# Fused q/k stack loads, a re-timed maxima chain and a new unit order in an attention + MLP kernel

## Chip, cores and metric

The kernel runs on one core of a Trainium2 chip. The metric is device time in microseconds (us), lower is better; the time of a kernel is the median over its runs. One further execution was recorded by the hardware profiler, and all rows of traces come from such an execution.

## The reference

For x of 2048 rows and 512 columns the kernel computes `g * a + (1 - g) * b`:

```
g = sigmoid((x * gate_w).sum(-1))
a = softmax(mask(q k^T / 4)) v @ wo      # q, k, v = x @ wqkv; 32 heads of 16 columns;
                                         # mask: row i sees rows i-255 .. i
b = gelu(layernorm(x) @ w1 + b1) @ w2 + b2   # w1: 512 x 1792, w2: 1792 x 512
```

## The kernel before

Every large matrix product is done in float32r (F32R) with operands split into a high part and a low remainder: `copy` (L121, on ACT) writes the high part, `lo_part` (L118, on DVE, or on POOL where asked for) the rest, and each product is three matmuls (high-high, low-high, high-low). PE is the engine of all matmuls.

Work runs in three phases.

**Phase one** makes q, k and v. `first_units` (PE L260) makes the first q and k block while its weights and x arrive; then a list of 48 *units* runs, one `tick` of a step counter for each: `qk_unit` (PE L272, 12 matmuls), one for each of 4 head groups, q or k and 4 blocks of 512 rows, and `v_unit` (PE L297, 12 matmuls), one for each of 16 blocks of 128 rows. `qk_out` splits each q or k result (ACT L121, DVE L118) and writes it to DRAM (`qkd`; L282 issued from ACT, L283 from SP). x is loaded in four blocks `load_x` (SP L216), the v weights by `load_wv` (SP L207). Beside the units the dictionary `plan` starts other things at unit numbers: `stat_unit` (row means and variances, DVE), `stat_end` (the reciprocal root by Newton steps, DVE), `load_y` and the first score blocks. `load_y` makes the normalised rows for the MLP, called y: for each half `cp` of the rows it loads 8 slices of 128x512, subtracts the mean and scales (L466, L467, on POOL), then splits (ACT L121, DVE L118). Before the change, the first half of y and half of the second are made in phase one, and four slices in phase two.

**Phase two** mixes attention with the MLP's first layer. The string `ORDER`, 1202 letters, is the program order of PE by hand: `S` is `s_pair`, scores for a block of 128 queries, two heads (PE L322), masked and reduced to row maxima by DVE (L328, or L331 and L332); `T` is `st_pair`, the transposed scores (PE L369), from which ACT takes the exponential (L371) and POOL clears what lies outside the window (`affine_select`, L373); `P` is `pv`, p times v (PE L388); `f` is one pair of matmuls of `mlp1_unit` (PE L578). Heads go by eight groups `p` of four, as two pairs `pr`; S runs six blocks (`LAG`) ahead of T. PE results of S, T, P and `mlp1_unit` share four double PSUM banks, handed round in turn (`ring`).

Two chains link these units through DRAM.

- *Stacks.* `load_stacks` (SP L309) brings 256 columns of q and k for head group p+1 from `qkd` into SBUF tiles `qs[0]`, `qs[1]`, `ks[0]`, `ks[1]`: four transfers of 98 partitions a call, 56 calls in phase two.
- *Maxima.* T needs minus the row maxima of S as two extra rows of the q stacks. After each fourth block `put_max` splits the maxima on POOL (L340 and L118, tile nm), transposes them on DVE (L345), writes them to a DRAM tile `md` (SP L346) and reads them back into the stacks (SP L353, four transfers). The split is issued at once, the transpose and the write at the next `tick`, the reads at the third; in phase two a `tick` is a `T` with `pr` 0.

DMAs are issued in program order from two queues, SP's and ACT's. The DMAs of both queues use eight completion semaphores in turn, and the issue of a DMA waits until the one that had its semaphore before is done.

**Phase three** (GELU on ACT L634, the MLP's second layer on PE L784, the output projection on PE L763, the gate on DVE L766 and L789) is not touched.

## Time and profile before

| | |
|---|---|
| runs before | 730.5, 727.93, 729.96 us; median 729.96 us |
| profiled execution | 728.15 us, its span 726.4 us, mean granted PE clock 0.995 |
| PE matmul busy | 699.0 us, 96% of the span |
| DVE, ACT, POOL busy | 472.7, 370.3, 281.1 us |
| phase one, two, three | first matmul at 6.23 us; first matmul of phase two at 156.17 us; last `P` at 510.77 us |
| DMA | 138.46 MB, mean 191 GB/s |

How to read it: busy PE time counts a matmul from its issue to its modelled end, and matmuls overlap, so 96% busy does not mean that PE runs at its best rate; what counts for a change is where PE stands idle, or issues more slowly than in a quiet stretch, and what it waited for. The granted clock (PEclk) is the share of the full TensorE clock that was granted in a stretch. Idle time of an engine other than PE costs nothing by itself.

### The profile page before, as it was taken

Reading aid. Unit: us, or ns where it says so; the run is one execution under the profiler, and the core shown is the slowest. Engines: PE = TensorE matmul, PEld = TensorE weight load, DVE = VectorE, ACT = ScalarE, POOL = GpSimd, SP = SyncE. Lnnn points to the kernel's source line nnn. Section 1 sums busy time; section 2 is a strip of 40 time slices with the busy share of each in tenths; the row PEclk is TensorE's granted clock in tenths of the full one; section 3 lists DMA queues with packets and bytes.
Section 4 is the critical chain, followed back from the end, with each engine's and each line's share of the span. In section 5 each row is a group of like instructions: output and inputs, shape, how many; then the busy total and the mean of one; then the engine's idle time right before and its main releaser. Section 6 shows DMA issues by size and latency. Waiting matters only on the chain.

```text
span 726.4 us, 16108 instructions
## 1 busy us (share of the span) xinstructions
PE 699.0 (96%) x5728; PEld 542.1 (75%) x5728; DVE 472.7 (65%) x981; ACT 370.3 (51%) x584; POOL 281.1 (39%) x612
## 2 busy tenths in 40 slices
...
GB/s 299 307 293 294 231 175 238 226 234 197 179 227 189 230 226 175 154 169 220 222 206 179 183 170 134 196 107 149 210 267 150 178 135 134 155 137 93 190 108 58
DMA packets 104675, 138.46 MB, mean 191 GB/s; under 512 B 15668, under 2 KB 55540, under 8 KB 104468
## 3 DMA queue, kind: packets, MB, share of 16 engines
...
## 4 chain that ended last, share of the span: by engine, by line
PE 78%; DMA 7%; DVE 5%; POOL 3%; SPq 2%; ACT 2%; issue 2%; ACTq 1%; DVEq 0%; POOLq 0%
PE ps_b L578 17%; PE ps_a L784 16%; PE ps_d L272 11%; PE ps_b L388 11%; PE ps_o L763 6%; PE ps_b L369 6%; PE ps_d L297 5%; PE ps_b L322 5%; DVE mx L332 2%; DMA qk<-t 2%; POOL p L373 2%; DVE ps_b L331 1%; DMA t<-in_w 1%; PE ps_d L260 1%; DMA hp<-t 1%
## 5 line engine op out<-in xcount | busy, mean ns | idle before, releaser
L373 POOL TENSOR_SCALAR_AFFINE_SELECT p<-p 128x256 f32<-128x256 f32 x480 | 184.2, 413 | 116.7 <-ACT p L371 115.0
L371 ACT ACTIVATE p<-ps_b 128x768 f32<-128x768 f32 (+2 forms) x256 | 191.3, 772 | 59.5 <-PE ps_b L369 51.7
L578 PE MATMUL ps_b<-x,w 64*128 64x512 f32 x1344 | 216.8, 398 | 0.5 <-DVE mx L332 0.4
L784 PE MATMUL ps_a<-x,t 128*128 128x512 f32 x648 | 154.6, 395 | 1.3 <-DVE t L638 1.2
L332 DVE TENSOR_REDUCE mx<-ps_b 128x2 f32<-128x512 f32 x208 | 144.1, 693 | 7.2
L784 PEld LDWEIGHTS ps_a<-x,t 128*128 128x128 f32 x648 | 121.4, 188 | 31.5 <-issue 1.6
L578 PEld LDWEIGHTS ps_b<-x,w 64*128 64x128 f32 x1344 | 132.7, 187 | 11.9 <-issue 3.6
L331 DVE COPY_PREDICATED ps_b<-tri,ps_b 128x256 f32<-128x256 uint8 x208 | 88.1, 424 | 54.9 <-PE ps_b L322 46.4
L369 PE MATMUL ps_b<-q,k 50*128 50x384 f32 (+5 forms) x512 | 91.8, 346 | 7.1 <-DVE mx L332 3.3
L272 PE MATMUL ps_d<-x,w 128*128 128x512 f32 x360 | 91.5, 404 | 3.7 <-ACT x L121 3.2
L388 PE MATMUL ps_b<-p,v 128*32 128x128 f32 (+1 forms) x1920 | 91.3, 329 | 0.7 <-ACT p L371 0.5
L322 PE MATMUL ps_b<-k,q 62*128 62x384 f32 (+2 forms) x472 | 86.9, 346 | 3.5 <-DVE mx L328 1.5
L272 PEld LDWEIGHTS ps_d<-x,w 128*128 128x128 f32 x360 | 67.9, 191 | 22.9 <-ACT x L121 4.6
L388 PEld LDWEIGHTS ps_b<-p,v 128*32 128x32 f32 x1920 | 54.1, 109 | 36.8 <-ACT p L371 4.8
L121 ACT ACTIVATE t<-ps_b 128x256 f32<-128x256 f32 (+1 forms) x114 | 52.9, 489 | 46.0 <-PE ps_b L388 35.6
L369 PEld LDWEIGHTS ps_b<-q,k 64*128 64x128 f32 (+1 forms) x512 | 52.0, 185 | 28.9 <-issue 14.4
L322 PEld LDWEIGHTS ps_b<-k,q 62*128 62x128 f32 x472 | 48.2, 186 | 17.5 <-ACT p L371 4.0
L118 DVE TENSOR_TENSOR t<-t,t 128x512 fp32r<-128x512 f32 x70 | 48.5, 692 | 14.9 <-ACT t L121 11.9
L634 ACT ACTIVATE t<-t,b1s 128x512 f32<-128x512 f32 x56 | 37.9, 715 | 25.5 <-DMA t<-hp 24.8
L121 ACT ACTIVATE t<-t 128x512 fp32r<-128x512 f32 x16 | 10.1, 632 | 76.7 <-DVE t L751 35.7
L763 PE MATMUL ps_o<-w,t 128*128 128x512 f32 x192 | 46.6, 392 | 0.6 <-ACT t L121 0.5
L297 PE MATMUL ps_d<-wv,x 128*128 128x512 f32 x192 | 46.9, 394 | 0.0
...
## 6 DMA issues: line engine op xcount, KB each, us to landing
...
k<-qk SPq DMA_DIRECT2D x112, 98.0 KB
q<-qk SPq DMA_DIRECT2D x112, 98.0 KB
...
```

Of the source, the lines that this page charges most:

```text
L272: pe.matmul(o, a[:, dt * 128:(dt + 1) * 128], b[:, dt * C:(dt + 1) * C], start=n == 0, stop=n == 11)
L297: pe.matmul(o, x[:, a:a + 128], wvs[dt][:, k], start=n == 0, stop=n == 11)
L322: pe.matmul(o[:, e, :n], qs[pr][r:k, qb * 128:qb * 128 + 128], ks[pr][r:k, t0:t0 + n], start=True, stop=True)
L331: dve.copy_predicated(o[:, :, :128], tri, o[:, :, 256:384])
L332: dve.tensor_reduce(m, o[:, :, :256], mybir.AxisListType.X, ALU.max)
L369: pe.matmul(o[:, e, :w], ks[pr][r:k, kb * 128:kb * 128 + 128], qs[pr][r:k, kb * 128:kb * 128 + w], start=True, stop=True)
L371: act.activation(pt[:, :, :w], o[:, :, :w], AF.Exp, scale=0.25)
L373: pool.affine_select(out=pt[:, :, a:a + 128], in_=pt[:, :, a:a + 128], pattern=[[0, 2], [sgn, 128]], base=b, channel_multiplier=-sgn, comp ...
L388: pe.matmul(a[32 * h:32 * h + 32, at:at + w], vs[:, kb, v:v + 32], pts[p, kb][:, h, fr:fr + w], start=n == 0, stop=n == len(parts) - 1, sk ...
L578: pe.matmul(o[:, e], w[kt // 4][r:r + 64, k, m:m + 128], y[r:r + 64, a:a + C], start=n == 0, stop=n == 23)
L763: pe.matmul(a, x[:, g], wos[g][:, k], start=n == 0, stop=n == 11)
L784: pe.matmul(accs[c][b], x[:, b * 128:(b + 1) * 128], w, start=f == 0 and n == 0, stop=f == FT - 1 and n == 2)
```

## The change

It does the following.

1. *Stacks in one tile.* The four stack tiles become one tile `qk` with four slots; `load_stacks` issues two transfers instead of four, each with both head pairs, and the maxima's reads become two instead of four.
2. *Maxima by order steps.* In phase two the four steps of `put_max` are issued 6, 11, 13 and 20 letters of `ORDER` after the `S` that completes a group of maxima (`CHAIN`, `soon`): split, transpose, write, read. In phase one they stay with the ticks.
3. *All of y in phase one.* `stat_end` is split into two halves at units 22 and 30; `load_y(0)` starts at unit 24 (31 before), `load_y(1)` with all eight slices at unit 33 (40 before, with four slices); the split of a slice comes one step later. The pool `x8` gets ten buffers instead of eight, and in phase two two of them serve as p tiles, whose pool shrinks from seven to five.
4. *Start.* The first weights come in three pieces (128, 128 and 256 columns) instead of two of 256, for q and k; twelve bf16 matmuls on a tile of zeros run on PE ahead of the first real ones; the split of x's third block (`rests[2]`), which was at unit 3, goes ahead of the first `qk_out`.
5. *Order.* `ORDER` is a new string with the same numbers of letters: 647 f, 256 T, 236 S and 63 P.
6. *Scratch.* The scratch for dynamic DMAs is halved.

The diff; of the two `ORDER` strings only the first line of each is shown, where `...` stands:

```diff
--- before.py
+++ after.py
@@ -35,20 +35,21 @@
 EPS = 1e-5
 NEG = -3.0e38
 U8 = mybir.dt.uint8
-ORDER = ("fSfTfffffTfTSfffSffTfSfffTTfffTfSfffSPSTSfffTTfffSfffTSfffTffSfTPTSffTffSffTSffSfSPTSTfffSffTfSffSPT"
...
+ORDER = ("fTSTffffffSffTfSfffTfSffTfSfffTSffffSPffSfffTSfffTfSffTfSfffTfffTSfTfffSffSPTTSPTSfffTfSffTfSfffTSff"
...
          "TT")
 LAG = 6
+CHAIN = (6, 11, 13, 20)
 
 
 @with_exitstack
@@ -131,19 +132,25 @@
         for fn in todo.pop(step[0], []):
             fn()
 
+    spot = [None]
+    soons = {}
+
+    def soon(n, fn):
+        soons.setdefault(spot[0] + n, []).append(fn)
+
     def settle():
         while todo:
             tick()
 
     osc = dram.tile([8, 128, S], F32, name="osc")
-    stat = dram.tile([2, S], F32, name="stat")
+    stat = dram.tile([2, 2, S // 2], F32, name="stat")
     hp = dram.tile([NCH, FT, 128, C], F32, name="hp")
     qkd = {(g, t): dram.tile([HG, 50, S], F32R, name=f"qk{g}_{t}") for g in range(NG) for t in range(2)}
 
     open_pool("w")
     open_pool("ring")
-    qs = [get("ring", f"q{j}", 1, (128, S), F32R) for j in range(2)]
-    ks = [get("ring", f"k{j}", 1, (128, S), F32R) for j in range(2)]
+    qk = get("ring", "qk", 1, (128, 4, S), F32R)
+    qs, ks = [qk[:, pr] for pr in range(2)], [qk[:, 2 + pr] for pr in range(2)]
     vs = get("ring", "v", 1, (128, NB, VR))
     tri = consts.tile([128, 2, 128], U8, name="tri")
     wide = consts.tile([128, 256], BF16, name="wide")
@@ -152,7 +159,7 @@
     g0 = consts.tile([128, NB], F32, name="g0")
     g1 = consts.tile([128, NB], F32, name="g1")
     mv = consts.tile([128, NB, 2], F32, name="mv")
-    rt = consts.tile([128, 2, NB], F32, name="rt")
+    rt = consts.tile([128, 2, 2, NB // 2], F32, name="rt")
 
     open_pool("edge", "right")
     get("edge", "edge", 1, (128, 8))
@@ -162,7 +169,7 @@
     gws = get("work", "gws", 1, (128, D))
 
     def x8():
-        return get("x", "x8", 8, (128, 2048), F32R)
+        return get("x", "x8", 10, (128, 2048), F32R)
 
     def wt():
         return get("w", "w", 6, (128, 2, 512), F32R)
@@ -186,6 +193,7 @@
         for e in range(2):
             pool.tensor_copy(tri[:, e], one[:, :128])
         pool.memset(wide, 0.0)
+        pool.memset(rt, 0.0)
         pool.affine_select(out=wide[:, 128:], in_=wide[:, 128:], pattern=[[-1, 128]], base=0, channel_multiplier=1,
                            compare_op=ALU.is_ge, fill=NEG)
 
@@ -238,18 +246,25 @@
             wq[0, t] = w
             ws.append(w)
             raws.append(t2())
-        for a in range(2):
+        pieces = (slice(0, 128), slice(128, 256), slice(256, 512))
+        for k in pieces:
             for t in range(2):
-                act.dma_start(raws[t][:, a * 256:a * 256 + 256], wqk[0, t, :, a * 256:a * 256 + 256])
+                act.dma_start(raws[t][:, k], wqk[0, t, :, k])
         _, hi, lo = load_x(0)
+        idle = t2()
+        dve.memset(idle, 0.0)
+        idle = idle.bitcast(BF16)
+        o = two()[:, 0]
+        for _ in range(12):
+            pe.matmul(o, idle[:, :128], idle[:, :512], start=True, stop=True)
         masks()
         loads()
         for t in range(2):
             os.append(ps("d"))
         for dt in range(DT):
             for t in range(2):
-                if dt % 2 == 0:
-                    k = slice(dt * 128, dt * 128 + 256)
+                if dt < 3:
+                    k = pieces[dt]
                     copy(ws[t][:, 0, k], raws[t][:, k])
                     lo_part(ws[t][:, 1, k], raws[t][:, k], ws[t][:, 0, k])
                 if t == 0:
@@ -260,6 +275,7 @@
                     pe.matmul(os[t], ws[t][:, k, dt * 128:dt * 128 + 128], x[:, dt * C:dt * C + C],
                               start=dt == 0 and n == 0, stop=dt == DT - 1 and n == 2)
         rests[1]()
+        rests[2]()
         for t in range(2):
             qk_out(0, t, 0, os[t])
 
@@ -303,10 +319,9 @@
     def load_stacks(p, a, n):
         g, j = divmod(p, 2)
         held_cols[p] = a + n
-        for pr in range(2):
-            for t, dst in ((1, ks[pr]), (0, qs[pr])):
-                src = view(qkd[g, t], [S, 98], [1, n], off=(4 * j + 2 * pr) * 50 * S + a)
-                sp.dma_start(f32(dst[14:112, a:a + n]), f32(src))
+        for t in (1, 0):
+            src = view(qkd[g, t], [S, 98], [100 * S, 2], [1, n], off=4 * j * 50 * S + a)
+            sp.dma_start(f32(qk[14:112, 2 * t:2 * t + 2, a:a + n]), f32(src))
 
     mxs, done = {}, set()
 
@@ -337,23 +352,31 @@
         mx = mxs[p][:, :, :, a:a + 4]
         m = small("nm", 2, (128, 2, 2, 2, 4), F32R)
         ms = small("ms", 2, (128, 32))
-        pool.tensor_copy(m[:, 0], mx)
-        lo_part(m[:, 1], mx, m[:, 0], pool)
         md = dram.tile([2, 2, 2, 4, 128], F32R, name=nm("md"))
+
+        def parts():
+            pool.tensor_copy(m[:, 0], mx)
+            lo_part(m[:, 1], mx, m[:, 0], pool)
 
         def turn():
             dve.transpose(ms, f32(m).rearrange("p a b c d -> p (a b c d)"))
+
+        def put():
             sp.dma_start(f32(view(md, [32, 4], [128, 32], [1, 32])), ms)
 
         def rest():
             done.add(("m", p, a // 4))
-            for pr in range(2):
-                for e in range(2):
-                    src = view(md, [2048, 2], [1, 512], off=(2 * pr + e) * 512)
-                    sp.dma_start(f32(qs[pr][62 + 50 * e:64 + 50 * e, a * 128:a * 128 + 512]), f32(src))
-
-        after(1, turn)
-        after(2 if (p, a) == (7, 12) else 3, rest)
+            for k in range(2):
+                src = view(md, [512, 2], [1024, 2], [1, 512], off=2048 * k)
+                sp.dma_start(f32(qk[62 + k:113 + k:50, :2, a * 128:a * 128 + 512]), f32(src))
+
+        if spot[0] is None:
+            parts()
+            after(1, lambda: (turn(), put()))
+            after(3, rest)
+        else:
+            for n, fn in zip(CHAIN, (parts, turn, put, rest)):
+                soon(n, fn)
 
     pts, acc = {}, {}
 
@@ -361,7 +384,7 @@
         w = min(NB - kb, 3) * 128
         assert ("m", p, (kb * 128 + w - 1) // 512) in done
         if pr == 0:
-            pts[p, kb] = get("work", "p", 7, (128, 4, 384))
+            pts[p, kb] = p_tile()
         pt = pts[p, kb][:, 2 * pr:2 * pr + 2]
         o = two()
         for e in range(2):
@@ -419,12 +442,13 @@
 
         after(3, rest)
 
-    def stat_end():
-        ve = small("ve", 1, (128, NB))
-        u = small("u", 1, (128, NB))
-        r = rt[:, 1, :]
+    def stat_end(half):
+        ve = small("ve", 2, (128, NB // 2))
+        u = small("u", 2, (128, NB // 2))
+        m = mv[:, half * 8:half * 8 + 8]
+        r = rt[:, half, 1]
         ri = r.bitcast(I32)
-        dve.tensor_scalar(ve, mv[:, :, 1], EPS, None, op0=ALU.add)
+        dve.tensor_scalar(ve, m[:, :, 1], EPS, None, op0=ALU.add)
         dve.tensor_scalar(ri, ve.bitcast(I32), 1, None, op0=ALU.logical_shift_right)
         dve.tensor_scalar(ri, ri, -1.0, float(0x5f3759df), op0=ALU.mult, op1=ALU.add)
         for _ in range(4):
@@ -432,10 +456,12 @@
             dve.tensor_tensor(out=u, in0=u, in1=ve, op=ALU.mult)
             dve.tensor_scalar(u, u, -0.5, 1.5, op0=ALU.mult, op1=ALU.add)
             dve.tensor_tensor(out=r, in0=r, in1=u, op=ALU.mult)
-        dve.tensor_copy(rt[:, 0, :], mv[:, :, 0])
+        dve.tensor_copy(rt[:, half, 0], m[:, :, 0])
         s = small("ms", 2, (128, 32))
-        dve.transpose(s, rt.rearrange("p a b -> p (a b)"))
+        dve.transpose(s, rt.rearrange("p h a b -> p (h a b)"))
         sp.dma_start(view(stat, [32, 4], [128, 32], [1, 32]), s)
+        if not half:
+            return
         for g, sgn in ((g0, -1.0), (g1, 1.0)):
             act.activation(g, z, AF.Exp, scale=sgn)
 
@@ -452,7 +478,7 @@
         mr = [t2() for _ in range(2)]
         for j in range(2):
             for e in range(2):
-                sp.dma_start(mr[j][64 * e:64 * e + 64], view(stat, [0, 64], [1, C], off=j * S + (2 * cp + e) * C))
+                sp.dma_start(mr[j][64 * e:64 * e + 64], view(stat, [0, 64], [1, C], off=cp * S + j * 2 * C + e * C))
 
         def one(s):
             if (cp, 0, s // 4) not in ys:
@@ -472,7 +498,7 @@
                 done.add(("y", cp, s))
 
             after(lag, rest)
-            after(lag + 2, fin)
+            after(lag + 3, fin)
 
         for s in range(s0, s1):
             after(1 + (s - s0) * gap // 2, lambda s=s: one(s))
@@ -519,7 +545,6 @@
     def at(n, fn):
         plan.setdefault(n, []).append(fn)
 
-    at(3, rests[2])
     for dt in range(DT):
         at(4 + dt // 2, rests["v"][dt])
     at(6, rests[3])
@@ -532,11 +557,12 @@
         at((4, 6, 8, 12)[c], lambda c=c: load_stacks(0, c * C, C))
     for i in range(NB):
         at(11 + i, lambda i=i: stat_unit(i))
-    at(30, stat_end)
+    at(22, lambda: stat_end(0))
+    at(30, lambda: stat_end(1))
     for n, (g, t) in enumerate((g, t) for g in range(1, NG) for t in range(2)):
         at((6, 7, 9, 10, 12, 13)[n], lambda g=g, t=t: after(3, load_w(g, t)))
-    at(31, lambda: load_y(0, 0, KT, 3, pool))
-    at(40, lambda: load_y(1, 0, KT // 2, 3, pool))
+    at(24, lambda: load_y(0, 0, KT, 3, pool))
+    at(33, lambda: load_y(1, 0, KT, 3, pool))
     at(41, lambda: load_w1(0, dve))
     at(44, lambda: load_w1(1, dve))
     for qb in range(NB - LAG):
@@ -556,12 +582,19 @@
     nt[0] = 9
     open_psum({"b0": 1, "b1": 1}, {"b2": 1, "b3": 1})
     ring += ["b0", "b1", "b2", "b3"]
+    extra = [f32(x8())[:, :1536].rearrange("p (h n) -> p h n", h=4) for _ in range(2)]
+    np_ = [0]
+
+    def p_tile():
+        np_[0] += 1
+        n = np_[0] % 7
+        return extra[n // 4] if n in (3, 6) else get("work", "p", 5, (128, 4, 384))
+
     late = []
 
     jobs = [(f, cp) for cp in range(2) for f in range(3)] + [(f, cp) for f in range(3, FT - 2) for cp in range(2)]
     jobs += [(f, cp) for cp in range(2) for f in range(FT - 2, FT)]
     load_w1(2)
-    after(1, lambda: load_y(1, KT // 2, KT, 2, pool, 4))
 
     def mlp1_unit(f, cp):
         held = ring.pop(0)
@@ -665,12 +698,16 @@
             early.extend(load_h(0, f) for f in range(2))
 
     early = []
+    spot[0] = 0
     lt = [(p, kb, pr) for p in range(8) for kb in range(NB) for pr in range(2)]
     ls = [(p, qb, pr) for p in range(8) for qb in range(NB) for pr in range(2)][2 * (NB - LAG):]
     lp = [(p, j) for p in range(8) for j in range(NB // 2)]
 
     def run(order):
         for a in order:
+            spot[0] += 1
+            for fn in soons.pop(spot[0], []):
+                fn()
             flush()
             if a == "T":
                 p, kb, pr = lt.pop(0)
@@ -818,7 +855,7 @@
 
 
 def build():
-    nc = bacc.Bacc("TRN2", target_bir_lowering=False, num_devices=1, dynamic_dma_scratch_size=1024)
+    nc = bacc.Bacc("TRN2", target_bir_lowering=False, num_devices=1, dynamic_dma_scratch_size=512)
 
     def inp(name, shape):
         return nc.dram_tensor(name, list(shape), F32, kind="ExternalInput").ap()
```

22 lines of the change are left out of this document (11 added, 11 removed).

## The prediction

> **What bounds the kernel now.** I read the page first, then stretches of phase two.
>
> ```profile
> span 726.4 us, 16108 instructions
> PE 699.0 (96%) x5728; PEld 542.1 (75%) x5728; DVE 472.7 (65%) x981; ACT 370.3 (51%) x584; POOL 281.1 (39%) x612
> ...
> 40.00:60.00 20.00, 20.00 (x89) 15.90 (x88) 7.52 (x20) 5.57 (x11) 3.55 (x2) 1.00 0.89 286
> 160.00:250.00 90.00, 82.85 (x960) 62.47 (x962) 65.36 (x148) 60.61 (x94) 61.30 (x144) 0.98 0.67 204
> 250.00:500.00 250.00, 246.56 (x3030) 189.72 (x3032) 185.32 (x416) 178.54 (x275) 147.82 (x392) 1.00 0.58 180
> 230.00:235.00 5.00, 2.50 (x14) 2.53 (x16) 1.12 (x2) 1.78 (x4) 3.00 (x6) 0.77 0.58 170
> 235.00:240.00 5.00, 5.00 (x61) 3.71 (x60) 2.92 (x7) 2.54 (x5) 1.93 (x7) 0.89 0.82 244
> ```
>
> PE is the bound: of 726.4 us it stands idle for 27.4. The change takes no real matmul away, so it can win only where PE idles or runs slowly. Phase one has no such place once it runs (20.00 of 20.00 busy from 40 to 60). The start has one (part 4). The first quarter of phase two is the other: from 160 to 250 PE idles 90 - 82.85 = 7.15 us; from 250 to 500 only 3.44 us, or 1.24 us for 90. So 5.9 us of idling are peculiar to the early stretch. Its granted clock is lower too: 5 x (1 - 0.77) + 5 x (1 - 0.89) = 1.70 us are lost between 230 and 240. Together 7.6 us. By matmuls the gap is larger: at the later pace (3030 in 250 us) 90 us would hold 1091, and 960 were issued; 131 missing at 12.1 per us are 10.8 us. So the early stretch offers 7.6 to 10.8 us.
>
> **Part 1: y leaves phase two.** The chain of waits from 155 to 190 us, by line:
>
> ```profile
> by line: POOL p L373 21.6%; DVE mx L332 12.9%; DVE x L118 8.3%; DVE ps_b L331 8.0%; POOL t L467 7.3%; POOL t L466 7.1%; issue 6.0%; PE ps_b L369 4.8%; PE ps_b L388 4.1%; PE ps_d L297 4.1%; POOL w L118 3.6%; PE ps_b L322 3.1%; PE ps_b L578 2
> ```
>
> PE has hardly a fifth of this chain. Scaling of y (L466, L467) and y's split (DVE x) hold 7.1 + 7.3 + 8.3 = 22.7% of 35 us, 7.9 us, ahead of the masking on which T and S wait. They go, with their four loads. PE cannot win all of it, since exponentials and maxima come next on the chain: it can win its 5.9 us of idling less the 2.9 of part 2, so 3.0, and by the matmul count up to 10.8 less the 4.6 of part 2, so 6.2. I take 4.5, the middle.
>
> The price is paid by DVE and POOL in phase one.
>
> ```profile
> 60.83 2.97 PE ps_d L272 x12
> 69.94 2.98 PE ps_d L272 x12
> ...
> L118 DVE TENSOR_TENSOR x<-t,x 128x512 fp32r<-128x512 f32 x5 | 8.1, 1636 | 1.1 <-ACT x L121 1.1
> L332 DVE TENSOR_REDUCE mx<-ps_x 128x2 f32<-128x512 f32 x4 | 2.8, 693 | 0.1
> L118 DVE TENSOR_TENSOR t<-ps_d,t 128x512 fp32r<-128x512 f32 x4 | 2.7, 686 | 5.1 <-ACT t L121 5.1
> L331 DVE COPY_PREDICATED ps_x<-tri,ps_x 128x256 f32<-128x256 uint8 x4 | 1.7, 419 | 0.0
> ```
>
> Three units and two score blocks take 69.94 - 60.83 = 9.11 us, a unit 3.04. The groups are DVE's from 120 to 140 us, while POOL works on y: y's split takes 1.64 us there, the same operation from PSUM 0.69. After the change a slice of y is due in each unit from 30 to 47, and DVE has for each 1.64 + 2/3 x 0.69 + 2/3 x (0.69 + 0.42) = 2.84 us of work in 3.04. It fits with 0.2 us to spare, and four PSUM banks of results hide a delay of two units. So nothing is charged; the second `stat_end` half, some twenty tiny DVE operations, has the same cover. If it is gone, see the rivals. y's twelve loads a half pass SP earlier, among the writes of q and k parts (L283) and the row loads of `stat_unit`; each waits for a free t tile, and behind it stand q and k writes that PE needs only in phase two.
>
> The Trainium skill's page "SBUF — State Buffer", section "Who interferes with whom", speaks against this move: a DVE instruction with two SBUF inputs and a GpSimd instruction that reads SBUF exclude each other. The trace agrees: 1636 ns against 686 ns with one input in PSUM.
>
> **Part 2: the maxima chain.** One group came late:
>
> ```profile
> 220.96 0.69 DVE L332 TENSOR_REDUCE mx<-ps_b 128x2 f32<-128x512 f32 x1
> 222.75 0.60 SPq L346 DMA_DIRECT2D md<-ms  x1
> 228.09 1.51 SPq L353 DMA_DIRECT2D q<-md  x4
> 232.50 0.68 PE L369 MATMUL ps_b<-q,k 64*128 64x384 f32 x2 [2.87 <-DMA q<-md]
> ...
> SPq L346 <- DVE ps_b L331: 29.6, 17, 5.1
> 156.17 0.50 PE L578 MATMUL ps_b<-x,w 64*128 64x512 f32 x2
> 510.77 1.72 PE ps_b L388 x32
> ```
>
> The maximum is done at 221.65 and its write issued at 222.75, but the reads only at 228.09, two ticks and a busy SP queue later; T waits 2.87 us. In the new order the reads stand seven letters behind the write. The 1202 letters take 510.77 - 156.17 = 354.6 us, 0.295 us each, so seven are 2.1 us instead of 5.3. The same T also stands 46 letters behind its S instead of 33 (counted in the strings). So the 2.9 us go, and the 1.7 us of low clock behind them: 4.6. What comes late next is ordinary bank waiting. The other steps move little: the split now queues behind a few `affine_select`s on POOL, the transpose is issued two letters ahead of the write, which shortens SP's 29.6 us of standing at L346 with all later transfers behind it. Those are off PE's path today. The reads, only 2.1 us behind the write, will often stand in SP until it has landed; behind them wait the results of the MLP (hp), w1 and the next stacks, for a microsecond or two that SP's fewer issues make good.
>
> **Part 3: half the stack transfers.**
>
> ```profile
> k<-qk SPq DMA_DIRECT2D x112, 98.0 KB
> 421.18 3.65 DMA q<-qk
> PE ps_b L322 <- DMA q<-qk: 0.5, 1, 0.5
> ```
>
> In phase two 112 stack issues and about 60 reads of maxima leave SP; bytes stay. PE waited only 0.5 us for a stack, so there is little to win, and the new order spends the room: from each `load_stacks` to the first S that needs it I add up letters (0.18 us for S and T, 0.23 for f, 1.44 for P, from the spacing of their matmuls). The shortest lead falls from 5.7 to 4.7 us, and 14 of 56 loads have at most 7 us (2 before). A load of half the size held the chain for 3.65 us: inside, not by much. I charge 0.5 us.
>
> **Part 4: the start.**
>
> ```profile
> 6.23 7.93 PE L260 MATMUL ps_d<-x,w 128*128 128x512 f32 x24 [6.23 <-ACT x L121]
> 22.95 8.24 PE L272 MATMUL ps_d<-x,w 128*128 128x512 f32 x24 [3.20 <-ACT x L121]
> 31.03 5.74 PE L297 MATMUL ps_d<-wv,x 128*128 128x512 f32 x24
> ...
> 22.27 2.19 ACT L121 ACTIVATE x<-v 128x512 fp32r<-128x512 f32 x4 [3.05 <-issue]
> 30.31 1.16 ACT L121 ACTIVATE wv<-t 128x512 fp32r<-128x512 f32 x2 [1.26 <-issue]
> ...
> 26.00:28.00 2.00, 2.00 (x6) 1.60 (x5) 0.17 (x2) 0.80 (x2) 0.00 (x0) 0.52 0.79 225
> ```
>
> Twenty-four matmuls take 5.74 us at 31.03, but 7.93 at 6.23, and 8.24 at 22.95, where the clock falls to 0.52 after a wait of 3.2. The dummies can give at most 7.93 - 5.74 = 2.2 us, the moved cast 3.2 + 8.24 - 5.74 = 5.7. But ACT is serial here: the v weights are split at 30.31 behind q and k copies and DMA issues, and PE takes them up at 31.03. An earlier PE waits there. ACT itself gains at most the 3.05 us that it lost at 22.27, less its standing for x's third block ahead of the first `qk_out`, which it delays. The finer first weights put two more issues on ACT, and two of x's first slices then wait for one of the eight semaphores; that may cost as much as the smaller first piece wins. So I take 1.5 us, the middle of 4 gained (3.05 and something of the dummies' 2.2) and 1 lost (two issues and a late slice).
>
> The Trainium skill ("TensorE: Matmul & The Clock Gate", Part 1) says that the clock is halved by default and freed by some 3.4 us of steady work. By that rule alone the dummies would bring their whole 2.2 us. The trace agrees in kind with the 0.52 after a wait.
>
> The halved scratch costs nothing: the DMA groups are issued by SP or ACT.
>
> **The sum**, against the profiled 728.15 us (the span and 1.75 around it): 4.5 (y) + 4.6 (maxima) - 0.5 (loads) + 1.5 (start) = 10.1 saved, 718.0. The median, 729.96, is 1.8 above that execution; I set the forecast of the median between, at 719.
>
> **Rivals.** *Everything pays in full*: 10.8 early in phase two, 4 at the start, 728.15 - 14.8 = 713. SP's 29.6 us of standing speak for it, ACT's serial start against. *DVE bounds phase one*, the SBUF page's rule taken at its word: if 18 units run 0.3 us over their 3.04, 5.4 us go back: 724. It decides once DVE needs more than 3.04 us a unit for longer than the banks cover. *Loads land late*, the slower side: if a double load needs 7 us, the 14 close ones stall 0 to 2.3 us, some 1.6 each, 22 us: 718 + 22 = 740. It begins where a landing passes 4.7 us; 3.65 at half size speaks against it, SP's standing for it. *The one tile ties what was apart*, so that transfers aren't really moved out of PE's way: if a load counts as covering all columns between its two halves, the next T waits for it, 56 x 3.65 = 204 us: 922. No row speaks for it.
>
> **How the numbers follow.** Forecast 0.55, full gain 0.15, DVE-bound 0.13, late loads 0.13, tied tile 0.04. Half a percent, 3.65 us, is about what a measurement can tell: faster means below 726.3. Forecast, full gain and most of DVE-bound lie there, 0.80; the mild end of late loads gives no change, 0.07; slower 0.13. The range of 710 to 729 holds the first three, with the ends of the early stretch and the start, and that mild end.
>
> **What would show it.** Right: from 160 to 250 PE idles about 2 us at clock 1.00; PE has no wait for q<-md; L466 and L467 end before phase two; the 1202 letters take about 346 us; the 3.2 us wait for x gives way to one for wv. Wrong: PE waits for q<-qk or k<-qk of over 5 us in sum; PE gaps on ps_d in units 30 to 47; a first matmul of phase two later than 156.17.

## The result, and the profile after

The changed kernel takes 747.7 us (median of 4 runs, 745.93 to 749.54) against 728.94 beside it: a ratio of 1.0256, 95% interval 1.0221 to 1.0292. The forecast was 719 and "faster". It is slower by 18.8 us, on the side to which the prediction gave 0.13; none of its rivals gives this time.

The page of the kernel after, and its busy time by stretches (us, then PE, PEld, DVE, ACT, POOL with their instructions, PE's granted clock, DMA share, GB/s):

```profile
span 746.6 us, 15926 instructions
PE 705.5 (94%) x5740; PEld 548.0 (73%) x5740; DVE 481.2 (64%) x1006; ACT 370.4 (50%) x585; POOL 280.8 (38%) x613
...
100.00:120.00 20.00, 15.38 (x57) 11.49 (x56) 12.71 (x24) 3.72 (x8) 11.97 (x9) 0.84 0.76 245
120.00:140.00 20.00, 15.61 (x61) 11.96 (x60) 18.39 (x41) 5.92 (x10) 9.28 (x10) 0.90 0.54 157
160.00:250.00 90.00, 88.17 (x956) 68.95 (x956) 64.90 (x144) 61.06 (x96) 49.59 (x123) 1.00 0.67 201
250.00:500.00 250.00, 238.43 (x2907) 184.70 (x2908) 180.52 (x408) 170.68 (x265) 141.82 (x377) 0.99 0.59 181
```

The same two stretches of phase one in the kernel before:

```profile
100.00:120.00 20.00, 20.00 (x90) 15.41 (x89) 14.43 (x46) 4.49 (x9) 1.41 (x3) 1.00 0.65 194
120.00:140.00 20.00, 20.00 (x90) 15.40 (x89) 13.75 (x17) 7.16 (x13) 19.45 (x15) 1.00 0.66 194
```

PE is idle 41.1 us instead of 27.4 (span less busy time). It idles in two new places of phase one, where before it never paused: 90 matmuls in 20 us became 57 and 61. From 250 to 500 its idling went from 3.44 to 11.57 us. What it waited for, longest sums first:

```profile
PE ps_x L337 <- DVE mx L347: 9.0, 4, 4.0
PE ps_b L392 <- DMA qk<-md: 8.7, 3, 4.5
PE ps_d L313 <- ACT wv L122: 6.6, 2, 4.6
PE ps_b L337 <- DMA qk<-qk: 6.2, 5, 2.5
```

Four places, one for each part of the prediction: banks of score blocks (ps_x) that DVE hadn't emptied in phase one (part 1), maxima read late (part 2), split v weights (part 4), stacks (part 3).

The profiled execution (748.36 us, against 728.15) is cut up below at the start of the thirteenth block of twelve matmuls ("start"), at phase two's first matmul, and at its last P. The later kernels are explained with their experiments.

| kernel | start | to phase two | the 1202 letters | rest |
|---|---|---|---|---|
| before | 48.5 | 107.7 | 354.6 | 215.7 |
| after | 51.6 | 121.7 | 358.5 | 214.8 |
| u_cast | 48.4 | 122.2 | 356.5 | 215.1 |
| early_stat | 50.9 | 108.2 | 359.7 | 214.4 |
| old_ticks | 51.0 | 123.5 | 348.6 | 213.9 |
| mix | 49.0 | 109.7 | 351.2 | 215.0 |
| s_new | 48.7 | 109.9 | 363.4 | 216.0 |
| s_letters | 48.2 | 111.3 | 360.7 | 213.9 |
| s_ticks | 48.7 | 110.1 | 363.7 | 215.0 |
| s_y | 47.9 | 109.4 | 353.6 | 213.3 |

So the 20.2 us of the two profiled executions are 3.1 (start) + 14.0 (the rest of phase one) + 3.9 (the letters) - 0.8 (the rest). Of the 14.0, 9.0 are the waits for ps_x; the lower clock of 100 to 140 us, 20 x (1 - 0.84) + 20 x (1 - 0.90) = 5.2 us, makes up the rest. Kernels with the order and the steps of the kernel after and all of y in phase one take from 356.5 (u_cast) to 366.3 us (short_lags, below) for the letters. One profile's figure in that column therefore says little below 10 us.

### The profile page after: what moved, and what is told of

Same layout as the page of the kernel before. It is cut to its first block, busy times and chain, and to the rows that moved or that the text cites. A ratio compares the mean times of both kernels' runs of the same rounds, so it can differ in the third digit from the quotient of the medians.

```text
span 746.6 us, 15926 instructions
## 1 busy us (share of the span) xinstructions
PE 705.5 (94%) x5740; PEld 548.0 (73%) x5740; DVE 481.2 (64%) x1006; ACT 370.4 (50%) x585; POOL 280.8 (38%) x613
## 4 chain that ended last, share of the span: by engine, by line
PE 74%; DMA 11%; DVE 6%; SPq 4%; ACT 2%; issue 1%; ACTq 1%; POOL 0%; DVEq 0%
PE ps_b L611 19%; PE ps_a L821 16%; PE ps_b L411 11%; PE ps_d L288 7%; PE ps_b L392 6%; PE ps_b L337 6%; PE ps_o L800 5%; PE ps_d L313 5%; DMA qk<-qk 4%; DMA t<-in_xa 2%; DMA qk<-md 1%; ACTq L298 1%; DMA v<-in_xt 1%; DMA md<-ms 1%; DMA hp<-t 1%
## 5 line engine op out<-in xcount | busy, mean ns | idle before, releaser
L396 POOL TENSOR_SCALAR_AFFINE_SELECT p<-p 128x256 f32<-128x256 f32 x344 | 131.7, 411 | 108.2 <-ACT p L394 97.6
L394 ACT ACTIVATE p<-ps_b 128x768 f32<-128x768 f32 (+2 forms) x184 | 137.5, 770 | 53.5 <-PE ps_b L392 49.7
L346 DVE COPY_PREDICATED ps_b<-tri,ps_b 128x256 f32<-128x256 uint8 x208 | 88.5, 425 | 68.0 <-PE ps_b L337 51.6
L392 PE MATMUL ps_b<-qk 64*128 64x384 f32 (+5 forms) x512 | 90.0, 342 | 8.9 <-DMA qk<-md 8.7
L337 PE MATMUL ps_b<-qk 62*128 62x384 f32 (+3 forms) x472 | 85.6, 344 | 7.6 <-DMA qk<-qk 6.2
L411 PE MATMUL ps_b<-p,v 128*32 128x256 f32 (+1 forms) x1376 | 74.6, 329 | 0.7 <-ACT p L394 0.7
L392 PEld LDWEIGHTS ps_b<-qk 64*128 64x128 f32 (+1 forms) x512 | 51.8, 186 | 25.8 <-issue 14.3
L396 POOL TENSOR_SCALAR_AFFINE_SELECT x<-x 128x256 f32<-128x256 f32 x136 | 52.3, 411 | 42.3 <-ACT x L394 41.3
L394 ACT ACTIVATE x<-ps_b 128x768 f32<-128x768 f32 (+2 forms) x72 | 54.8, 777 | 18.5 <-PE ps_b L392 11.5
L337 PEld LDWEIGHTS ps_b<-qk 62*128 62x128 f32 (+1 forms) x472 | 47.5, 186 | 21.7 <-issue 11.0
L119 DVE TENSOR_TENSOR t<-t,t 128x512 fp32r<-128x512 f32 x70 | 48.5, 693 | 14.6 <-ACT t L122 10.9
L313 PE MATMUL ps_d<-wv,x 128*128 128x512 f32 x192 | 50.9, 417 | 6.6 <-ACT wv L122 6.6
L313 PEld LDWEIGHTS ps_d<-wv,x 128*128 128x128 f32 x192 | 38.6, 202 | 17.0 <-ACT wv L122 8.0
```

What stands on the lines that cost most here:

```text
L313: pe.matmul(o, x[:, a:a + 128], wvs[dt][:, k], start=n == 0, stop=n == 11)
L337: pe.matmul(o[:, e, :n], qs[pr][r:k, qb * 128:qb * 128 + 128], ks[pr][r:k, t0:t0 + n], start=True, stop=True)
L346: dve.copy_predicated(o[:, :, :128], tri, o[:, :, 256:384])
L392: pe.matmul(o[:, e, :w], ks[pr][r:k, kb * 128:kb * 128 + 128], qs[pr][r:k, kb * 128:kb * 128 + w], start=True, stop=True)
L394: act.activation(pt[:, :, :w], o[:, :, :w], AF.Exp, scale=0.25)
L396: pool.affine_select(out=pt[:, :, a:a + 128], in_=pt[:, :, a:a + 128], pattern=[[0, 2], [sgn, 128]], base=b, channel_multiplier=-sgn, comp ...
```

## The experiments

Line numbers shift by a few between kernels. Eleven kernels have a single run each. The time of the kernel before that was measured beside it is 727.84 (u_cast, u_start, u_y, sp_first), 725.44 (short_lags, ticks, four, old_order) or a median of 727.49 (early_stat, old_ticks, wide).

### Undo one part of the start, or y's schedule

`u_cast` puts the cast of x's third block back:

```
         rests[1]()
-        rests[2]()
...
+    at(3, rests[2])
```

> The changed kernel with the cast of x's third block (rests[2]) back at unit 3; all else as changed. In the changed kernel the seventh block of twelve matmuls starts 1.9 us earlier than before the change, and the eighth 3.2 us later, which then stays. Theory A (the moved cast delays the first q and k writes on ACT, PE runs ahead, waits 4.6 and 2.0 us for the v weights and then runs at half clock): the 3.2 us go, and with the dummies' gain the eighth block starts 0 to 1 us ahead of before; the first matmul of phase two comes 3 to 4 us earlier than 173.3, about 169.7; total 744.5. Rival B (the finer first weights and the two more issues on ACT cost it): the eighth block stays about 3 us late, phase two starts at 173, total 748.

Measured 743.89. PE in the kernel after:

```profile
7.28 6.08 PE L275 MATMUL ps_d<-x,w 128*128 128x512 f32 x24 [1.59 <-ACT x L122]
13.20 11.36 PE L288 MATMUL ps_d<-x,w 128*128 128x512 f32 x48
29.12 1.32 PE L313 MATMUL ps_d<-wv,x 128*128 128x512 f32 x2 [4.56 <-ACT wv L122]
32.44 8.20 PE L313 MATMUL ps_d<-wv,x 128*128 128x512 f32 x22 [2.00 <-ACT wv L122]
```

and in u_cast:

```profile
7.24 6.07 PE L275 MATMUL ps_d<-x,w 128*128 128x512 f32 x24 [1.29 <-ACT x L122]
23.20 8.54 PE L287 MATMUL ps_d<-x,w 128*128 128x512 f32 x24 [4.28 <-ACT x L122]
31.57 5.75 PE L312 MATMUL ps_d<-wv,x 128*128 128x512 f32 x24
```

With the cast moved up, PE runs 48 matmuls through (13.20 to 24.56), then stands 4.56 and 2.00 us for the v weights, and the 22 matmuls behind that take 8.20 us where 24 take 5.75 (the granted clock was 0.50 from 32.4 to 36.5). The wait has moved behind the next block and grown from 4.3 to 6.6 us. Why the weights come late is in ACT's row of work in the kernel after:

```profile
17.11 1.25 ACTq L298 DMA_DIRECT2D qk<-t  x2
...
24.89 3.50 ACTq L298 DMA_DIRECT2D qk<-t  x2
28.44 1.15 ACT L122 ACTIVATE wv<-t 128x512 fp32r<-128x512 f32 x2 [3.58 <-DMA qk<-t]
...
31.76 1.15 ACT L122 ACTIVATE wv<-t 128x512 fp32r<-128x512 f32 x2 [1.69 <-issue]
```

ACT casts first, so its first q and k writes go out at 17.11; in u_cast they do so at 14.13. Then two issues stand 3.50 us until an earlier transfer lands, and the second half of the weights is split at 31.76 instead of 30.85 in u_cast (30.31 in the kernel before). In this pair the cast alone costs the 3.1 us of the start. Over all profiles the start is 49.3 to 51.6 us in the ten kernels with the cast moved up and 47.9 to 50.5 in the nine with it back, so its price is 2 to 3 us.

`u_start` undoes the dummies and the finer first pieces as well.

```
-        for _ in range(12):
-            pe.matmul(o, idle[:, :128], idle[:, :512], start=True, stop=True)
-        pieces = (slice(0, 128), slice(128, 256), slice(256, 512))
+        pieces = (slice(0, 256), slice(256, 512))
```

> The changed kernel with the whole start of before: cast at unit 3, weights in two pieces, no dummy matmuls. Theory A: start as before the change, so phase two begins 3.1 us earlier than 173.3, at 170.2, total 745.2; the other losses (14.1 us in units 31 to 35 and some 4 in phase two) stay. By rival B the same. Against the kernel with the cast alone undone it shows what dummies and pieces are worth: 0 to 1 us lost here.

Measured 749.61; start 48.3 against 48.4 of u_cast. The dummies do shorten the first block (6.07 us; 7.86 without them), but with the finer pieces it begins at 7.24 instead of 6.31. At the start they are together worth nothing. The run as a whole is 5.7 us above u_cast's, in phase one (123.5) and the letters (360.2), which the edit doesn't touch; that is within the spread of such single runs.

`u_y` has y's schedule of the kernel before, the last four slices in phase two, and a slice's split a tick sooner, as before.

```
-    at(22, lambda: stat_end(0))
-    at(30, lambda: stat_end(1))
+    at(30, lambda: [stat_end(half) for half in range(2)])
-    at(24, lambda: load_y(0, 0, KT, 3, pool))
-    at(33, lambda: load_y(1, 0, KT, 3, pool))
+    at(31, lambda: load_y(0, 0, KT, 3, pool))
+    at(40, lambda: load_y(1, 0, KT // 2, 3, pool))
...
+    after(1, lambda: load_y(1, KT // 2, KT, 2, pool, 4))
```

> The changed kernel with y's schedule of before: both stat_end halves at unit 30, load_y(0) at 31, half of load_y(1) at 40 and its other half in phase two. The 14.1 us that units 31 to 35 lose should go by either theory of them, so phase two begins at about 159.2; the four slices in phase two cost what they cost before, 3 to 6 us, so phase two's order takes 361 to 365 us instead of 358.5; total about 738. If y's schedule isn't the cause, phase two begins at 173.

Measured 747.37: phase one from the thirteenth block takes 108.8 again, so y's schedule holds the 14.0 us. But the letters take 370.6, more than the 361 to 365 expected, and PE waits 11.9 us for maxima. By these two profiles y in phase two costs 12 us in the new order, of which the spread can be much; in the old order it is less (s_y, below).

### What stalls phase one

`sp_first` moves the first finishing half of the statistics and y's first loads:

```
-    at(22, lambda: stat_end(0))
+    at(27, lambda: stat_end(0))
-    at(24, lambda: load_y(0, 0, KT, 3, pool))
+    at(28, lambda: load_y(0, 0, KT, 3, pool))
```

> The changed kernel with all of y still in phase one, but the first half's stat_end at unit 27 instead of 22 and load_y(0) at 28 instead of 24, so that SP comes to the write of the statistics only when all row loads of stat_unit have been issued. Theory Y-A (SP stands at that write behind DVE, the row loads behind it come late, DVE starves and then falls behind): most of the 14.1 us go, at most 4 left; phase two begins at 160 to 164, total 735 to 739. Rival Y-B (DVE and POOL exclude each other on y, DVE has simply too much to do in the later units): the loss stays or grows, since the slices now stand closer together; phase two begins at 171 to 176, total 746 to 751.

Measured 747.52, phase one 115.7: 6.0 of the 14.0 us are gone, less than theory Y-A asks and more than Y-B allows. The total is no lower because the letters took 363.9 us. SP in the kernel after:

```profile
83.66 0.54 SPq L434 DMA_DIRECT2D t<-in_xa  x1
88.48 0.55 SPq L462 DMA_DIRECT2D stat<-ms  x1
92.72 0.53 SPq L365 DMA_DIRECT2D md<-ms  x1
...
96.93 3.88 SPq L481 DMA_DIRECT2D t<-stat  x4
```

The write of the statistics (L462) stands from 84.2 to 88.5 for DVE's chain of tiny operations. Behind it stands the write of maxima, issued at 92.72, and from 96.93 the four reads of the statistics take 3.88 us of the queue. The row loads of `stat_unit` (L434) queue in between, and DVE, in order, waits for them. DVE in the kernel after, the second half of the statistics with it:

```profile
84.30 0.17 DVE L451 TENSOR_SCALAR ve<-mv 128x8 f32<-128x8 f32 x1
...
109.41 0.69 DVE L438 BATCH_NORM_STATS2 st<-t 128x6 f32<-128x512 f32 x1 [2.85 <-DMA t<-in_xa]
...
116.41 1.23 DVE L451 TENSOR_SCALAR ve<-mv 128x8 f32<-128x8 f32 x1
117.67 0.17 DVE L452 TENSOR_SCALAR rt<-ve 128x8 int32<-128x8 int32 x1
117.88 1.13 DVE L453 TENSOR_SCALAR rt<-rt 128x8 int32<-128x8 int32 x1
...
126.39 0.21 DVE L461 STREAM_TRANSPOSE ms<-rt 128x32 f32<-128x32 f32 x1
```

and PE, which then can't get a bank:

```profile
112.95 0.44 PE L337 MATMUL ps_x<-qk 62*128 62x384 f32 x2 [4.00 <-DVE mx L347]
...
129.66 0.44 PE L337 MATMUL ps_x<-qk 62*128 62x384 f32 x2 [3.76 <-DVE mx L347]
```

So the first stand of 4.00 us comes behind the late row loads, the second of 3.76 behind the second half of the statistics. The twenty operations on 8 columns ahead of the transpose took 3.9 us in the first half (84.30 to 88.24), and 10.0 in the second (116.41 to 126.39), while GpSimd (POOL in the rows) works on y:

```profile
115.89 1.72 POOL L492 TENSOR_TENSOR t<-t,t 128x512 f32<-128x512 f32 x1
117.69 1.29 POOL L493 TENSOR_TENSOR t<-t,t 128x512 f32<-128x512 f32 x1
```

The operation of 1.23 us ends at 117.64, GpSimd's at 117.61; the next slow one at 119.01, GpSimd's at 118.98. Six of the twenty took 1.13 to 1.23 us, and each ended within 0.04 us of the end of a GpSimd operation. The others, which began in a gap between two of these or after the last at 124.22, took 0.17. In sp_first two of the second twenty were slow, and they took 5.9 us; behind them PE still stood 2.7 us for ps_x.

`short_lags`, from sp_first, lets tiles be freed sooner, in case these are what is short.

```
-        after(3, rest)
+        after(2, rest)
-    at(28, lambda: load_y(0, 0, KT, 3, pool))
-    at(33, lambda: load_y(1, 0, KT, 3, pool))
+    at(28, lambda: load_y(0, 0, KT, 2, pool))
+    at(34, lambda: load_y(1, 0, KT, 2, pool))
-            after(lag + 3, fin)
+            after(lag + 2, fin)
```

> As the kernel with stat_end at unit 27 and load_y(0) at 28, but each row load of stat_unit is used two units after its issue instead of three, each slice of y is scaled two units after its load instead of three and split two later instead of three, and load_y(1) starts at 34. A slice then holds its t tile for five units instead of seven. In the kernel it is made from, units 12 to 48 still took 8.0 us more than before the change, and SP stood 8.8 us at a load of y whose t tile POOL had not freed. Theory Y-C (the 15 t tiles are all in use, so loads wait for tiles and SP stands with the q and k writes behind it, whose own t tiles then come late): 4 us or more of the 8.0 go; units 12 to 48 take 108 to 112 us instead of 115.7. Rival Y-B (DVE and POOL exclude each other and DVE has too much to do): nothing goes, 114 to 118 us.

Measured 751.51, phase one 118.2: 2.5 us worse than sp_first, and DVE waits 9.3 us for row loads (2.2 in sp_first). Tiles are not shown to be what is short.

`early_stat` takes both suspects away: statistics three units earlier, both finishing halves in unit 27, ahead of y.

```
-        at(11 + i, lambda i=i: stat_unit(i))
+        at(8 + i, lambda i=i: stat_unit(i))
-    at(22, lambda: stat_end(0))
-    at(30, lambda: stat_end(1))
+    at(27, lambda: [stat_end(half) for half in range(2)])
-    at(24, lambda: load_y(0, 0, KT, 3, pool))
-    at(33, lambda: load_y(1, 0, KT, 3, pool))
+    at(28, lambda: load_y(0, 0, KT, 3, pool))
+    at(35, lambda: load_y(1, 0, KT, 3, pool))
```

The constants are loaded four units earlier with them, and `fin` follows a tick sooner; all 16 slices stay in phase one.

> The changed kernel with all of y still in phase one, but statistics done before y begins: the row loads of stat_unit start at unit 8 instead of 11, both stat_end halves run at unit 27, load_y(0) starts at 28, load_y(1) at 35, and a slice's split comes one unit earlier. Theory Y-D (two things cost the 14.1 us: DVE starves while SP stands at the early write of the statistics with row loads behind it, and the second stat_end's twenty tiny operations take up to 1.2 us each, because POOL works on y beside them): both are gone, units 12 to 48 take 107.5 to 110 us, against 107.7 before and 121.7 in the changed kernel; total 733 to 736. Rival Y-B (too much DVE and POOL work in the last 17 units, now that y is pressed into them): 113 us and more, with gaps behind unit 36.

Measured 734.8, phase one 108.2 (107.7 before). Its busy time in the two stretches:

```profile
100.00:120.00 20.00, 20.00 (x87) 15.35 (x88) 12.57 (x46) 4.29 (x8) 4.85 (x4) 1.00 0.65 199
120.00:140.00 20.00, 20.00 (x90) 15.39 (x89) 13.58 (x19) 6.53 (x11) 19.45 (x16) 1.00 0.66 204
```

PE has no pause left, with as much y in phase one as in the kernel after, so the amount of y is not what stalled it. Both suspects are gone: DVE waits 0.2 us for row loads, and GpSimd touches y only from 113.61, when the forty operations of the two halves, each of at most 0.17 us, are over (105.1). The run moves y's starts and the split too, and doesn't part these from the statistics; the traces above tie PE's two stands to late row loads and slow statistics.

### What the letters, the order and the halved transfers are worth

`ticks` puts the maxima's steps back on ticks, in the new order; `old_order` keeps the letters (for the last group 2, 6, 8 and 14, since the old order leaves no more) and puts the old order back; `old_ticks` does both; `four` has four transfers a load again; `wide` puts reads twelve letters behind the write instead of seven:

```
ticks:
-            for n, fn in zip(CHAIN, (parts, turn, put, rest)):
-                soon(n, fn)
+        parts()
+        after(1, lambda: (turn(), put()))
+        after(2 if (p, a) == (7, 12) else 3, rest)
four:
-        for t in (1, 0):
-            src = view(qkd[g, t], [S, 98], [100 * S, 2], [1, n], off=4 * j * 50 * S + a)
-            sp.dma_start(f32(qk[14:112, 2 * t:2 * t + 2, a:a + n]), f32(src))
+        for pr in range(2):
+            for t, dst in ((1, ks[pr]), (0, qs[pr])):
+                src = view(qkd[g, t], [S, 98], [1, n], off=(4 * j + 2 * pr) * 50 * S + a)
+                sp.dma_start(f32(dst[14:112, a:a + n]), f32(src))
wide:
-CHAIN = (6, 11, 13, 20)
+CHAIN = (4, 6, 8, 20)
```

old_order has the string of the kernel before as ORDER; four also reads the maxima in four transfers; wide takes 2, 4, 6 and 14 for the last group.

> The changed kernel with the maxima's steps of before, in phase two too: split at once, transpose and write at the next tick, reads at the third. Theory M-A (the write reaches SP late and the reads stand right behind it for its landing, 40.8 us of SP in all, so that groups of maxima come late): waits of PE for maxima fall from 8.7 us to under 4 and SP's standing for md's landing to under 10, phase two's order takes 3 to 6 us less than 358.5. Rival M-B (the new order is what makes them late, by the SP work it puts in between): the waits stay at 8 or rise, the order takes 358 to 364.

> The changed kernel with four transfers again in each stack load and each read of maxima, in the one tile. Theory L-A (the double loads land later, and the new order's short leads are for loads of half the size): the 6.2 us for which PE waited for stacks fall under 2, phase two's order takes 4 us less than 358.5. Rival L-B (SP's issues are what is short): PE's waits for stacks and maxima rise above 15 us together, the order takes 362 or more.

> The changed kernel with the letters of the order of before; the maxima's steps still come by letters, 6, 11, 13 and 20 behind their S, for the very last group 2, 6, 8 and 14, since there only 19 letters lie between. Theory O-A (the new order's tight leads cost what is lost in phase two): PE's waits for stacks go under 1 us, for maxima under 5; the order takes 348 to 353 us, since y is gone from it. Rival O-B (the letters for the maxima and SP's standing cost it in any order): waits for maxima of 8 us and more, the order takes 356 to 362.

> The changed kernel with the order of before and the maxima's steps of before (ticks); stacks in one tile, half the transfers, all of y in phase one and the new start stay. The order of before alone gave 355.5 us for phase two's order, the ticks alone 355.1, the changed kernel 358.5, the kernel before (with four slices of y in it) 354.6. Theory P-A (letters and order each cost 3 us and more, and without both the gain from y shows): 345 to 350 us, PE's waits for maxima and stacks under 4 us together. Rival P-B (moving y out gains nothing, or the double transfers cost what it gains): 353 to 357.

> The changed kernel with the maxima's steps at 4, 6, 8 and 20 letters instead of 6, 11, 13 and 20 (2, 4, 6, 14 for the last group). The reads then stand twelve letters, 3.5 us, behind the write instead of seven, 2.1 us; a write took 3.4 us to land where SP waited for it. Theory M-C (SP's standing for md's landing, 40.8 us, makes the rest late): standing falls under 15 us, PE's waits for maxima under 4 and for stacks under 4, the order takes 353 to 356 us. Rival M-D (standing only changes its place: SP waits for the transposes instead, and the groups stay late): waits as in the changed kernel, 357 to 360 us.

Measured 742.12, 754.39, 742.04, 738.69 and 744.95; the letters in 355.1, 362.3, 355.5, 348.6 and 355.7 us. Against the spread of 356.5 to 366.3 only old_ticks stands out: undoing letters and order together brings about 10 us. Four transfers don't help the new order. In wide SP stands 19.4 us for the write's landing instead of 40.8, and PE waits 4.6 us for maxima instead of 8.7, but the 2.8 us that the letters gain are within the spread. Because phase one was late by 14 us in all of these, with loads done while PE stood, the comparison was made again on a sound phase one.

`mix` joins the edits of early_stat, u_cast, old_order and ticks shown above; all y in phase one, halved transfers and the dummies stay.

> What the runs so far point to: the changed kernel with its cast moved back, statistics done before y begins (as in the run with early row loads), and order and maxima's steps of before. What is left of the change: one stack tile with half the transfers, all of y in phase one, dummies and finer first weights. If the causes found are the whole story, the start is 0 us off before, phase one 0 to 2 us, and phase two gains what y held there, 5 to 9 us: 719 to 725 us, faster than before by 0.5 to 1.2%. If y's four slices were hidden in phase two or the double transfers cost something: 727 to 731, no difference.

Measured 728.07 (median of 10) against 727.49: ratio 1.0022 [0.9991, 1.0053], no difference, so the gain of 5 to 9 us that the expectation names first didn't come. From it, one edit of phase two at a time: `s_letters` (the letters again), `s_ticks` (the new order again), `s_new` (both), `s_y` (the lines of u_y for y and the statistics).

> The same with the order string of the kernel before, the steps still by letters (2, 6, 8 and 14 for the last group). Differs from the version with both undone by the letters alone. Theory L (a read seven letters behind a write that takes 3.4 us to land makes the queue stand, whatever the order): SP stands 40 us or more for maxima, letters in 354 to 358 us, 3 to 6 us slower than the 728.1 of the version with both undone, so 731 to 734. Rival (letters are harmless in the old order): 728, within 0.3% of it.

> The same with the new order and the steps by ticks as before. Differs from the version with both undone by the order alone. Theory O (the new order puts more loads close to their use and is worse by itself): letters in 354 to 358 us, 731 to 734. Rival (the order is worth nothing either way once maxima come by ticks): 727 to 729.

> The kernel after with a sound phase one (statistics three units earlier, both finishing halves at unit 27) and the cast back at unit 3; phase two's instructions are wholly those of the change: new order, the maxima's steps by letters, no y in it. Theory G (the letters and the new order each lose about what y's leaving gains, so that all the edits of phase two together are worth nothing or a small loss): 1202 letters in 356 to 361 us, time 731 to 735, 0.5 to 1% above the kernel before. Rival H (phase two only looked bad because a late phase one left it late rows of q and k; with a sound phase one it gains what the prediction said): letters in about 347 us, time 720 to 724, below the kernel before.

> Old order, steps by ticks, cast at unit 3, and y scheduled as before with its last four slices in phase two: of the change there stay the halved transfers, the finer first weights with the dummies, and the tiles. Theory G says that y's leaving is worth 3 to 6 us in phase two in the old order and costs about 2 in phase one as placed in the version with both undone: letters in 354 to 357 us, first matmul of phase two 107.5 to 108.5 us behind the 13th block, time 728 to 731. Rival Y0 (y's last slices are hidden in the old order; what gained 3.4 us there were the halved transfers): letters in 350 to 352, time 725 to 727, faster than the kernel before.

| | median | ratio to the kernel before (729.01) |
|---|---|---|
| s_letters | 735.95 | 1.0089 [1.0057, 1.0121] |
| s_ticks | 739.01 | 1.0123 [1.0096, 1.0150] |
| s_new | 739.21 | 1.0131 [1.0096, 1.0167] |
| s_y | 728.13 | 0.9977 [0.9953, 1.0000] |

By the ratios, beside mix's 1.0022, the letters cost 0.7% or 5 us, the order 1.0% or 7 us, and both together hardly more than the order; with the intervals of two ratios each figure may be off by 3 us. The rival that phase two had only looked bad behind a late phase one falls: with a sound one, s_new's letters take 363.4 us, longer than any theory had it.

What PE waits for in phase two of s_ticks,

```profile
PE ps_b L387 <- DMA qk<-md: 6.5, 4, 2.5
PE ps_b L336 <- DMA qk<-qk: 4.5, 5, 1.8
```

and of mix:

```profile
PE ps_b L387 <- ACT v L122: 2.9, 1, 2.9
PE ps_b L387 <- DMA qk<-md: 1.6, 3, 1.0
PE ps_b L336 <- DMA qk<-qk: 1.3, 1, 1.3
```

11.0 us against 2.9 for maxima and stacks: in the new order both come too late, also when the maxima's steps are those of before.

For maxima the order's own leads are the likely reason. Counted in the strings, the T that needs a group of maxima stands 33 letters behind the S that completes it for the group that was late before the change, and 46 in the new order; there PE no longer waits. But for the second group of head group p = 2 the distance falls from 46 to 37, and for that of p = 5 from 44 to 37. At the T of the first of these PE waits 4.54, 4.84, 5.25 and 5.59 us in after, u_cast, early_stat and s_new, and 1.22 in s_ticks; at that of the second 0.7 to 2.5 us in these five; in mix at neither. Where new order and steps by letters come together, the last group has 23 letters for a chain that itself takes 20, and PE waits 1.1 to 3.3 us there in the first four.

For stacks the double loads are slower to land. This is the one in the kernel after that PE waited longest for (2.50 us), in the chain of work, with its start and the time to its landing:

```profile
334.44 5.66 DMA qk<-qk
```

The other four waits there are for loads of 6.59, 5.01, 3.94 and 5.59 us. Half-size loads on the chain of work took 3.57 and 3.65 us before the change and 3.93 to 4.87 in `four`. Four of the five loads are among the 14 that the prediction counted with at most 7 us.

The letters move SP's standing. SP's own waits in s_letters, and in mix:

```profile
SPq L370 <- DMA md<-ms: 39.1, 25, 4.6
```

```profile
SPq L370 <- DMA md<-ms: 9.5, 13, 1.8
```

In the kernel before it stood 3.1 us so. But at the write of the maxima SP stands 48.5 us in s_letters and 78.9 in mix, and with the reads 87.6 against 88.4: the sum is the same, and the standing by itself is not shown to be the loss. What PE shows is that the maxima come later:

```profile
PE ps_b L391 <- DMA qk<-md: 5.6, 5, 2.0
```

That is 5.6 us in s_letters against 1.6 in mix, 4.0 more, beside a cost of 5 us by the ratios. A place where this ends on PE, in the timeline of the kernel after:

```profile
258.84 0.20 DVE L362 STREAM_TRANSPOSE ms<-nm 128x32 f32<-128x32 f32 x1
...
260.40 1.79 SPq L324 DMA_DIRECT2D qk<-qk  x2
...
262.29 0.61 SPq L365 DMA_DIRECT2D md<-ms  x1
...
267.71 1.38 SPq L371 DMA_DIRECT2D qk<-md  x2
...
271.94 0.69 PE L392 MATMUL ps_b<-qk 64*128 64x384 f32 x2 [4.54 <-DMA qk<-md]
```

The transposed maxima are ready at 259.04, but their write goes out 3.2 us later behind other issues, the reads 5.4 us after that, and T, which stands at a fixed letter, waits 4.54 us. A place in the order is a time only as long as SP isn't late.

`s_y` against `mix` shows what y is worth. In s_y the 65th T starts 96.1 us after the first (98.3 before), in mix 91.2: y's absence gives 4.9 us early in phase two. The other profiles in the old order with ticks agree: 96.0 and 96.5 with y there (best and best4, below; best has mix's statistics), 91.3 without (old_ticks). But mix's first T starts 3.8 us into phase two and s_y's 0.8. PE in mix:

```profile
158.64 0.50 PE L606 MATMUL ps_b<-x,w 64*128 64x512 f32 x2
...
162.45 0.69 PE L387 MATMUL ps_b<-qk 64*128 64x384 f32 x2 [2.90 <-ACT v L122]
```

and ACT in mix, with three of the y copies ahead of the last copy of v:

```profile
154.44 0.63 ACT L122 ACTIVATE x<-t 128x512 fp32r<-128x512 f32 x1 [1.76 <-POOL t L488]
...
157.85 0.63 ACT L122 ACTIVATE x<-t 128x512 fp32r<-128x512 f32 x1 [2.30 <-POOL t L488]
...
160.77 0.63 ACT L122 ACTIVATE x<-t 128x512 fp32r<-128x512 f32 x1 [1.79 <-POOL t L488]
```

GpSimd hands over a slice every 2.9 to 3.4 us; it is not through when phase one ends, and ACT, standing for it, holds up v. 3.0 of the 4.9 us go back there. In whole runs the gain doesn't show: mix is at 1.0022 [0.9991, 1.0053], s_y at 0.9977 [0.9953, 1.0000].

Two last runs aim at a version that beats both. `best` is s_y with early_stat's statistics, `best4` the same with the four transfers of `four`:

```
-    at(31, lambda: load_y(0, 0, KT, 3, pool))
-    at(40, lambda: load_y(1, 0, KT // 2, 3, pool))
+    at(28, lambda: load_y(0, 0, KT, 3, pool))
+    at(37, lambda: load_y(1, 0, KT // 2, 3, pool))
```

> Old order, steps by ticks, halved transfers, finer first weights with the dummies, cast at unit 3; statistics three units earlier, y's first twelve slices from units 28 and 37, its last four in phase two as before. In the version with all of y in phase one PE stands 2.90 us behind ACT's copy of v at the start of phase two, since ACT stands in front of y's copies that GpSimd hands over only every 3.4 us, against 2.9 us a unit. Theory P (GpSimd sets y's pace, so the last slices cannot go into phase one for nothing): without them that stand is gone, as with y's old schedule, and the earlier statistics shorten phase one by 1 to 2 us against that schedule: 725 to 728, a ratio of 0.993 to 0.998. Rival (the earlier statistics are worth nothing once y has its old schedule): 728, ratio 0.998 to 1.002.

> The same with the four transfers a stack load and four reads of maxima of the kernel before. Theory Q (halving them gives SP's queue room, and so 1 to 3 us early in phase two, where the kernel before waits for maxima): 1 to 3 us slower than with two, 727 to 730. Rival (the prediction's: room in SP was not short in the old order): within 1 us of the version with two.

Measured 730.02 and 729.61 against 730.28: ratios 0.9986 [0.9969, 1.0004] and 0.9999 [0.9975, 1.0022]. PE's wait for v is gone in both, as theory P has it, but the earlier statistics bring nothing (phase one 110.1), and halving the transfers is worth less than can be told. No version was shown to beat the kernel before; s_y comes nearest.

## Why the prediction was wrong

**Its frame held.** PE is the bound, and the places it named (start, end of phase one, early phase two) are where the time moved. It failed in what it charged for the moves. It had 1.5 us gained at the start, nothing lost in the rest of phase one and 8.6 gained in the letters (4.5 + 4.6 - 0.5); the profiles have 3.1, 14.0 and 3.9 lost.

**Part 1, y leaves phase two.** The 4.5 us came out in the stretch that it meant: 4.9 measured, mix against s_y. That it is so near is in part luck, since 4.5 was the middle of 3.0 and 6.2, and 3.0 of it went back at the boundary. The step that failed is "nothing is charged". Steady work did fit: in early_stat all 16 slices pass beside a PE that never pauses, so the rival of DVE as the bound falls in the form given. What the step passed over: (a) it named SP's queue for y's loads, with the row loads among them, but not the statistics' write, which stands there for DVE, and counted only what PE needs in phase two; the row loads, which DVE needs at once, came late; (b) the second finishing half, "some twenty tiny DVE operations", was given the cover of ordinary work, and took 10.0 us instead of 3.9. The cover itself was miscounted: the four banks are those of q, k and v (ps_d), while all four waits were for the banks of score blocks (ps_x), of which phase one has two. Together 14.0 us, and nearly all of it gone with early_stat (108.2 against 107.7). (c) POOL's pace was never compared with a unit's 3.04 us: 3.0 us at the boundary. The Trainium skill's page "SBUF — State Buffer", section "Who interferes with whom", named the cause of (b) in kind, GpSimd and DVE excluding each other; the trace agrees, at 1.1 to 1.23 us for an operation of 0.17. The prediction had applied it only to y's own large operations.

**Part 2, the maxima chain.** Forecast 4.6 gained; the letters cost 5 us (s_letters against mix), and PE waited 8.7 us for maxima in the kernel after where it had waited 2.9. Two steps failed. The first looks at the one late group (33 letters to 46) and calls what comes next "ordinary bank waiting": that group was cured by its 46 letters (in s_letters, with the old order, it still waits 1.67), but others came closer (46 to 37), and PE stood there instead, 4.54 us. The second is that reads standing in SP would hold what is behind them "for a microsecond or two that SP's fewer issues make good": SP stood 40.8 us in 25 waits at the reads, and fewer issues made none of it good (`best4` against `best` tells no gain from halving). How much of the 5 us is this standing stays open, since in mix SP stands as long, at the write. In the old order with ticks the letters take 351.2 us, of which 3.0 are the wait for v: about 348, near the 346 that the prediction wanted from the new order and the letters.

**Part 3, half the transfers.** Charged 0.5 us for stacks that come closer to their use. The kernel after waited 6.2 us for them, and the order as a whole, of which that is one effect, costs about 7 (s_ticks against mix). The figures were there: a shortest lead of 4.7 us, 14 of 56 within 7. The late-loads rival put 22 us on that and had the mechanism, with a size that was too large; it was set aside because one half-size load took 3.65. That is the step that failed: the double loads that PE waited for took 3.94 to 6.59 us, four of the five over the 4.7 at which that rival begins.

**Part 4, the start.** 1.5 us gained was forecast, 3.1 lost. The prediction said that an earlier PE would wait for the v weights, and that the first `qk_out` would be delayed, but took that for less gain. That is the step that failed; it is a loss, because the delayed writes stand in ACT's own queue and push the weights behind where they were. The dummies' bound of 2.2 us came out as 1.8, of which the finer pieces took back 0.9 at the first matmul, and the rest didn't reach the thirteenth block.

**The signs to look for** were partly met. L466 and L467's work did leave phase two, but PE waits 8.7 us for maxima, not 0, and the letters take 358.5, not 346. Of the three signs given for wrong all came: stack waits of 6.2 us in sum, a first matmul of phase two at 173.31, and gaps of PE in units 31 and 34, though on ps_x and not on ps_d as written. The wait for x did give way to one for wv, and from 160 to 250 PE idles only 1.83 us at clock 1.00; both were signs for right and neither made time: the first is the start's loss, and the second stretch begins 13 us before phase two now does.

**What stays open.** Why the edits of letters and order don't add (5 and 7, together 7 to 8 us); how much of the new order's 7 us its shorter leads cost (PE's waits for maxima and stacks are 8.1 us more than in mix) and what else does, such as its places for P; and why mix and its kin need 109.4 to 111.3 us for phase one from the thirteenth block where before needs 107.7, early_stat 108.2.
